# The first loads by pairs of heads, ten more idle products, and a new written order for the opening of an attention and feed-forward kernel

## The chip, the core and the metric

The kernel runs on one core of a Trainium2 chip. The core has five engines that each work through a queue of instructions in order: TensorE (PE, with its weight loads as PEld), VectorE (DVE), ScalarE (ACT), GpSimd (POOL), and SyncE (SP), which here only issues transfers. They meet through semaphores. The metric is the device time of one execution in microseconds (us), the median of several runs.

## The reference

Eight batches, eight heads, 576 tokens of 64 numbers. k and v are first averaged over groups of 8 tokens, so that each head has 72 keys and values. Behind the attention stands a feed-forward layer with a gate.

```python
k_p = k.reshape(B, H, 72, 8, D).mean(axis=3);  v_p = likewise
scores = (1 / sqrt(D)) * q @ k_p^T
attn = exp(scores - max);  attn = attn / (sum(attn) + 1e-9)
x = (attn @ v_p), heads side by side: 4608 tokens x 512
h = x @ w_in                      # 512 x 2048
g = h * clip(h + 3, 0, 6) / 6
out = g @ w_out                   # 2048 x 512
```

## The kernel before, in words

The 4608 tokens are cut into ten blocks (512, 256, 384, six of 512, 384). For a block, the feed-forward layer runs in 16 steps `f`, one for each 128 of the 2048 inner columns: `Step.h` (L782) forms h in PSUM, ScalarE and VectorE apply the gate (`relu`, `gate` L794, `hi`, `lo`), and `Step.out` (L813) adds the step's part of the result. Each product is split into high and low parts, three matmuls for one. While a block's steps run, the attention of the next block is laid between them. So almost all of the run is a stream of matmuls, and only the opening, in which the attention of block 0 is made with nothing to lay it beside, is different.

**The opening.** Block 0 is the first 512 tokens of batch 0, four tiles of 128 tokens: A is the tiles 0 and 128, B the tiles 256 and 384. Heads are taken in four pairs, and two pairs make a group `g` (0 or 1), so a tile has two sets of scores, 4 heads by 72 keys each.

- `load_first` issues the loads: four k of a pair each (L257), q of tile 0 and of tile 128 (L259), the 8 remaining keys' v (`vr`, L260), v of pairs 0 and 1 and of pairs 2 and 3 (L262), the two halves of the weights of step 0 (L653), and q of tokens 256 to 511 (L264) between these. Then come the weights of step 1, the k of batch 1 (`load_k`, L200), and, in `load_second`, batch 1's v (L375) and its remainder three times over (L377).
- `prep_k` (L214) sums 8 tokens of k on VectorE; ScalarE scales the sums into `kbd` (L222). The same function serves batch 1 with another `kbd`.
- `busy` (L270) forms idle products of the identity, which nothing reads: 13 ahead of the scores and 3 behind them.
- `FirstValues.heads` (L290) sums 8 tokens of v by products with the identity, 16 products; `FirstValues.rest` (L301, L303) does the remainder on GpSimd.
- `Scores`: `product` (L412) on TensorE; `top` (L416), the maximum, on VectorE; `exps` (L420), four exponentials with their sums, on ScalarE. The fourth set of A has `shift` (L427) and `total` (L433) on VectorE and one wide `exp` (L430) on ScalarE instead. `invert` (L436, L437) on VectorE; `divide` (L448, L454) on GpSimd or VectorE.
- `transposes_of_half` (L507, L509): six transposes of the weights for two tiles and one g, then a copy of the main part out of PSUM (L510, VectorE or ScalarE) and of the remainder (L511, ScalarE).
- `av` (L583): the product with the values for a pair of heads, then the split into `xhi` (L588) and `xlo` (L589).
- `prep(f, ...)`: the weights of a step are made out of 64-bit words: `scale` (L695) and `low` (L684) on ScalarE, `sign` (L689) and `join` (L700) on VectorE, `hi` (L723) on ScalarE, `lo` (L728) on VectorE. Those of steps 0, 1 and 2 fall into the opening.
- `pool_second` (L385) sums batch 1's v on VectorE, six instructions.

**What sets the order.** `ORDER` is a table: for each engine, the numbers of its instructions of the opening and the first steps behind it, in the order in which the engine is to run them (a number is the place of the instruction in the order of the program's text; for SP they are the loads). `put_in_order` chains them by `behind`, which adds an order with no semaphore. Each engine then takes its instructions strictly in that order; waits between engines follow from the data and the buffers.

On TensorE, the order before is: 13 idle products; the scores of A in the order tile 0 of g 1, tile 0 and tile 128 of g 0, tile 128 of g 1; 3 idle products; the value sums; transposes of g 0; the first scores of B; transposes of g 1; `av` of A; further scores of B between products of step 0; transposes and `av` of B, whose third product is the `av` at 34.07 us.

Of the kernel before, what the change touches and what calls it, by code (L numbers as in the profile page):

```python
# [17 lines left out]
P = 128  # L18
# [12 lines left out]

ORDER = {
    "PE": """
        0-12 17-18 13-16 19-45 50-53 56-57 46-49 54-55 60-63 58-59 64-68 78-79 69-71 80-85 88-89 72-74 86-87
        75-77 100-101 96-99 102-108 118-126 109-111 211-214 112-117 93-95 90-92 127-144 230-233 145-147 246-247
        148-156 166-171 157-159 163-165 266-267 160-162 193-195 184-189 172-180 190-192 196-198 181-183 218-223
        199-201 208-210 277-278 297-298 202-204 299 215-217 205-207 224-229 251-253 240-242 234-236 248-250
        243-245 237-239 254-259 279-281 260-262 268-270 263-265 274-276 315-316 282-287 306-308 288-296 334-336
        303-305 271-273 300-302 309-314 323-328 317-322 337-342 349-350 362-364 331-333 343-345 329-330 346-348
        354-356 365-367 357-359 368-376 385-387 360-361 380-381 351-353 382-384 388-390 377-379 391-393 419-421  # L40
        394-396 400-402 409-411 397-398 406-408 403-405 422-427 451-453 438-440 428-430 399 441-443 454-456
        431-433 416-418 457-462 444-446 412-415 479-481 466-468 434-437 476-478 469-472 447-450 463-465 482-493
        473-475 536-537 503-505 494-496 530-532 562-563 544-546 497-499 547-549 533-535 538-540 582-583 541-543
        500-502 512-514 509-511 550-555 515-517 506-508 556-558 518-523 576-578 559-561 564-569 579-581 524-526
        584-589 570-572 527-529 573-575
    """,
    "DVE": """
        3 2 1 0 4-8 87 11 15 9 12 17 16 10 18 13 19 14 20-21 23 22 24 26 34 28 40 64 29 25 61 32 30 33 62 36 35
        37 27 39 38 47 31 43-44 41 65 55 93 45 50 49 51 63 52-53 56 54 42 48 59-60 57-58 99 74 46 100 77 73 106
        76 75 79 81 78 82 111 80 107 121 86 108 83-84 112 67 110 85 113 90 88 109 89 68 94 114 91-92 115 131 96  # L50
        98 95 101 136 97 103 66 143 105 102 116 104 137 118 117 132 122 120 126 119 128 133 127 130 129 144 140
        123 138 147 139 142 141 72 149 145 70-71 146 124 69 152 125 135 148 151 150 154 156 134 159 153 157 155
        166 158 160-161 168 170 167 163 172 162 169 173 164-165 171 174-175 178-179 187 183 181 184-186 188 194
        176 189 182 177 190 199 191 180 200 192 201 193 195 197-198 202 196 203
    """,
    "Activation": """
        3 2 0-1 4-18 27 19 34 21 20 25 23 82 22 24 81 28-32 35-38 46 26 33 53 40-43 54 44 47-50 52 56 51 60 55
        39 59 69 89 61 57-58 45 88 74 96 95 71 67 70 75 68 97 104-107 98 72 76 79 73 80 77 108-111 86 78 83-84
        93 62 90 85 87 94 117-120 91 126-129 99 102 92 115 103 100 112 136 65 130 137 101 138-139 116 113 124
        121 114 125 122 140 123 143 66 63 131 64 132 134 144 135 153 133 145 141 147 142 150 148 146 154 151 149  # L60
        155 157 160 156 152 166 158 161 159 167 170-172 162-163 168 164 173 165 174 176 178 169 175 183 177
        180-181 179 187 186 184 188 185 194-197 189 202-205 198-199 182 200 208-211 190-191 201 206 192 207
        212-213 193
    """,
    "Pool": """
        0-1 12 2-3 18 4 7-8 10 5 9 6 14 13 16 15 17 11 19-20 24 21 23 22
    """,
    "SP": """
        2-3 1 0 4-5 8 6-7 14 9 11 10 22-24 21 20 13 12 15 18 16 19 25-26 28 31 17 27 32 34 33 29 41 30 44 51 35
        48 46 43 36 47 39 52 59 42 37-38 45 40 50 49 53-55 57-58 60 56  # L70
    """,
}

# [2 lines left out]
def attention_moe_kernel(  # L76
# [19 lines left out]
    nc = tc.nc  # L96
    NB, _, NPAIR, S = q.shape
# [5 lines left out]
    NG = NPAIR // 2  # L103
# [7 lines left out]
    for j, t in enumerate(starts):  # L111
        end, mine = t + BLOCKS[j], []
# [83 lines left out]
    kraw = {}  # L196
# [48 lines left out]
    def load_first():  # L245

        st = [stage(i) for i in range(16)]
        qs = [st[i].rearrange("p (c t) -> p c t", c=NPAIR) for i in (11, 4)]
        pieces[256], pieces[0] = [st[1:4], 0], [st[8:11], 0]
        vraw[0] = stages[3].rearrange("p a (c n) -> p (a c) n", a=2, c=NPAIR // 2)  # L250
        vraw[0, NPAIR] = st[5][:REM].rearrange("p (g n) -> p g n", g=NG)
        for t in tiles_of[0]:
            _, s0, _, _ = t[0]
            qtiles[t] = [qs[s0 // 256][:, :, s0 % 256 : s0 % 256 + P]]
        for p in range(NPAIR):
            kraw[0, p] = st[12 + p][:, :S]
            nc.sync.dma_start(kraw[0, p], k[0, p])  # L257
        for o in range(0, 256, P):
            nc.sync.dma_start(qs[0][:, :, o : o + P], q[0, :, :, o : o + P])  # L259
        nc.sync.dma_start(vraw[0, NPAIR], vr[0].rearrange("g r n -> r g n"))  # L260
        for p in range(0, NPAIR, 2):
            nc.sync.dma_start(vraw[0][:, p : p + 2], v[0, p : p + 2].rearrange("p r n -> r p n"))  # L262
        load_w(0, slice(0, 1))
        nc.sync.dma_start(qs[1], q[0, :, :, 256:512])  # L264
        load_w(0, slice(1, 2))

    def busy(n):

        for _ in range(n):
            nc.tensor.matmul(idle, ident, ident, start=True, stop=True)  # L270
# [585 lines left out]

    window.append(len(traced))
    load_first()
    load_w(1)
    for p in range(NPAIR):  # L860
# [237 lines left out]
```

## Time and profile before

| | us |
|---|---|
| median of 3 runs | 923.84 |
| the runs | 923.11 to 926.03 |
| the profiled execution | 923.03 |
| its span | 921.2 |
| TensorE busy | 908.1 (99%) |
| VectorE busy | 457.4 (50%) |
| ScalarE busy | 461.7 (50%) |
| GpSimd busy | 82.0 (9%) |

The span is the time from the first to the last instruction that the profiler saw; the run's own time is 1.8 us more. TensorE's share hides the opening: of the span's 40 slices (23 us each) only the first two and the last have TensorE under 90%.

### The profile page before, as it was taken

The page shows a single profiled execution, that of the slowest core. Times are in us where ns is not written, and L with a number is a line of the kernel's source. Part 1 is how long each engine was busy: PE and PEld are TensorE (multiplying, and loading weights), DVE is VectorE, ACT ScalarE, POOL GpSimd, SP SyncE. Part 2 cuts the span into 40 slices and gives each one's busy share as a digit, 9 for nine tenths or more (in the row PEclk, how much of TensorE's full clock was granted, in tenths as well). Part 3 has the DMA queues.
Part 4 walks back from the last instruction along what each step waited for, and adds up shares of the span by engine and source line. Part 5 has one row for each costly group of instructions (what it writes and reads, how often), then busy time and mean ns, then how long its engine had stood idle before and what let it go on. Part 6 is the DMA issues. An engine that isn't in the chain of part 4 may idle for free.

```text
span 921.2 us, 12671 instructions
## 1 busy us (share of the span) xinstructions
PE 908.1 (99%) x4548; PEld 776.8 (84%) x4548; DVE 457.4 (50%) x916; ACT 461.7 (50%) x1340; POOL 82.0 (9%) x167
## 2 busy tenths in 40 slices
PE   7899999999999999999999999999999999999998
PEld 7688889999888888888888888888888888888997
DVE  6999855475356333824356326633356234332322
ACT  6898665465355434633456335633545344333322
POOL 4100001021000100101011101110101001100000
PEclk9999999999999999999999999999999999999999
DMA  9960203050031002300042004100210010000100
GB/s 313 393 242 1 92 12 121 1 166 19 0 115 58 24 1 80 104 12 6 1 145 57 12 1 134 61 12 1 92 42 23 1 41 18 0 1 3 45 1 35
DMA packets 41935, 57.19 MB, mean 62 GB/s; under 512 B 7568, under 2 KB 23696, under 8 KB 41872
## 3 DMA queue, kind: packets, MB, share of 16 engines
q1 hardware_dynamic: 41728, 56.37, 19.0%
q8 instruction: 36, 0.59, 0.3%
q14 instruction: 27, 0.22, 0.1%
q10 hardware_dynamic: 144, 0.00, 0.0%
HBM read 46.93 MB, written 9.44 MB: 61 GB/s over the span
## 4 chain that ended last, share of the span: by engine, by line
PE 96%; DVE 2%; DMA 1%; SPq 0%; ACT 0%; issue 0%; DVEq 0%
PE pso L813 43%; PE psh L782 43%; PE psa L583 4%; PE psa L412 4%; PE psa L518 2%; DMA kst<-k_l 1%; PE psa L520 0%; DVE u L689 0%; ACT stage L420 0%; DVE u L700 0%; SPq L257 0%; DVE stage L448 0%; SPq L259 0%; DVE a L510 0%; SPq L262 0%
## 5 line engine op out<-in xcount | busy, mean ns | idle before, releaser
L782 PE MATMUL psh<-xhi,w 128*128 128x512 f32 (+2 forms) x1288 | 402.3, 372 | 0.0
L813 PE MATMUL pso<-w,ghi 128*128 128x512 f32 (+1 forms) x1184 | 367.0, 391 | 0.0
L782 PEld LDWEIGHTS psh<-xhi,w 128*128 128x128 f32 x1288 | 238.0, 188 | 36.1 <-issue 0.4
L813 PEld LDWEIGHTS pso<-w,ghi 128*128 128x128 f32 x1184 | 214.1, 188 | 36.0
L782 PE MATMUL psh<-xlo,w 128*128 128x512 f32 (+2 forms) x644 | 237.5, 369 | 0.0
L794 DVE SCALAR_TENSOR_TENSOR g<-g,psh 128x512 f32<-128x512 f32 (+2 forms) x161 | 101.4, 630 | 271.6 <-ACT g L790 270.4
L813 PE MATMUL pso<-w,glo 128*128 128x512 f32 (+1 forms) x592 | 225.9, 386 | 0.0
L790 ACT ACTIVATE g<-psh,small 128x512 f32<-128x512 f32 (+2 forms) x161 | 103.7, 644 | 209.7 <-PE psh L782 193.3
L782 PEld LDWEIGHTS psh<-xlo,w 128*128 128x128 f32 x644 | 121.3, 188 | 18.2
L802 DVE TENSOR_TENSOR glo<-g,ghi 128x512 fp32r<-128x512 f32 (+2 forms) x161 | 102.7, 638 | 62.1 <-ACT ghi L798 60.2
L813 PEld LDWEIGHTS pso<-w,glo 128*128 128x128 f32 x592 | 111.1, 188 | 21.7
L798 ACT CAST ghi<-g 128x512 fp32r<-128x512 f32 (+2 forms) x161 | 92.9, 577 | 70.6 <-DVE g L794 67.9
L420 ACT ACTIVATE e<-psa,mx 128x72 f32<-128x72 f32 x256 | 78.5, 322 | 50.8 <-DVE mx L416 50.1
L448 POOL TENSOR_TENSOR a<-e,sm 128x256 f32<-128x256 f32 x60 | 41.2, 687 | 517.2 <-PE pso L813 180.3
L420 ACT ACTIVATION_READ_ACCUMULATOR e<-psa,mx 128x1 f32 x256 | 52.8, 206 | 0.0
L416 DVE TENSOR_REDUCE mx<-psa 128x4 f32<-128x288 f32 x72 | 32.3, 454 | 29.2 <-PE psa L412 28.8
L412 PEld LDWEIGHTS psa<-kbd,qt 128*128 128x128 f32 x288 | 43.1, 189 | 4.2
L412 PE MATMUL psa<-kbd,qt 128*128 128x144 f32 x288 | 45.5, 285 | 0.0
L585 ACT COPY x<-psa 128x192 f32<-128x192 f32 (+7 forms) x60 | 23.0, 387 | 32.6 <-PE psa L583 32.4
L332 DVE TENSOR_REDUCE vsum<-vst 128x64 f32<-128x512 f32 (+1 forms) x36 | 37.8, 1068 | 2.3 <-DMA vst<-v_l 1.5
L436 DVE TENSOR_SCALAR sm<-sm 128x4 f32<-128x4 f32 x72 | 12.4, 176 | 48.7 <-ACT e L420 45.7
L529 ACT CAST ahi<-psa 128x256 fp32r<-128x256 f32 (+1 forms) x70 | 24.6, 353 | 18.8 <-PE psa L518 9.8
(93 smaller groups left out, 628.9 us busy)
## 6 DMA issues: line engine op xcount, KB each, us to landing
out<-o SPq DMA_DIRECT2D x35, 256.0 KB, 2.3
raw<-w_in_l SPq DMA_DIRECT2D x16, 512.0 KB, 8.4
raw<-w_out_l SPq DMA_DIRECT2D x16, 512.0 KB, 9.1
kst<-k_l SPq DMA_DIRECT2D x28, 288.0 KB, 3.2
qt<-q_l SPq DMA_DIRECT2D x28, 256.0 KB, 3.2
vst<-v_l SPq DMA_DIRECT2D x24, 256.0 KB, 3.0
vst<-vr_l SPq DMA_DIRECT2D x36, 64.0 KB, 1.9
stage<-k_l SPq DMA_DIRECT2D x4, 288.0 KB, 3.6
```

The lines of the kernel that those rows point to most:

```text
L332: nc.vector.tensor_reduce(out=vs[:n, p], in_=st[:n, : POOL * D].rearrange("p (o d) -> p d o", o=POOL), axis=AX.X, op=ALU.add)
L412: nc.tensor.matmul(to, qt[:, p, :], kbds[b % 2][:, p, :], start=r == 0, stop=r == last)
L416: nc.vector.tensor_reduce(out=self.mx, in_=self.ps, axis=AX.X, op=ALU.max, negate=True)
L420: nc.scalar.activation(self.e[:, h], self.ps[:, h], AF.Exp, bias=self.mx[:, h : h + 1], accum_out=self.sm[:, h : h + 1])
L448: engine.tensor_tensor(out=self.a[:, : 4 * D].rearrange("p (h s) -> p h s", h=4), in0=e[:, :, :D], in1=sm[:, :, None].broadcast_to([P, 4, D]),
L583: nc.tensor.matmul(ps, l, r, start=n == 0, stop=n == len(mms) - 1)
L782: nc.tensor.matmul(self.ps, l[f][:, c, :], r[:, c, :], start=c == 0 and i == 0, stop=c == NCC - 1 and i == 2)
L790: nc.scalar.activation(self.g, self.ps, AF.Relu, bias=half, scale=1.0 / (6.0 * WSCALE))
L794: nc.vector.scalar_tensor_tensor(out=g, in0=g, scalar=1.0, in1=self.ps, op0=ALU.min, op1=ALU.mult)
L798: nc.scalar.copy(self.ghi, self.g)
L802: nc.vector.tensor_tensor(out=self.glo, in0=self.g, in1=self.ghi.bitcast(F32), op=ALU.subtract)
L813: nc.tensor.matmul(pos, l, r[:, cols], start=f == 0 and i == 0, stop=f == NF - 1 and i == 2)
```

## The change

`load_first` takes q of the first 256 tokens by heads, where it took it by tokens: the k of pairs 0 and 1, the q of these pairs for all 256 tokens, the k of pairs 2 and 3, their q. The second `busy` makes 13 idle products where it made 3. And the whole table `ORDER` is another.

```diff
-        for p in range(NPAIR):
-            kraw[0, p] = st[12 + p][:, :S]
-            nc.sync.dma_start(kraw[0, p], k[0, p])
-        for o in range(0, 256, P):
-            nc.sync.dma_start(qs[0][:, :, o : o + P], q[0, :, :, o : o + P])
+        for g in range(NG):
+            mine = slice(2 * g, 2 * g + 2)
+            for p in range(NPAIR)[mine]:
+                kraw[0, p] = st[12 + p][:, :S]
+                nc.sync.dma_start(kraw[0, p], k[0, p])
+            nc.sync.dma_start(qs[0][:, mine], q[0, :, mine, :256])
...
     values.rest()
-    busy(3)
+    busy(13)
...
     "PE": """
-        0-12 17-18 13-16 19-45 50-53 56-57 46-49 54-55 60-63 58-59 64-68 78-79 69-71 80-85 88-89 72-74 86-87
+        0-12 15-16 21 13-14 22-23 17-18 24 19-20 25-26 34-49 54-55 50-53 64-65 68-69 56-59 62-63 76-78 66-67
+        60-61 88-89 27-28 74-75 70-71 29 72-73 90-93 30 79-84 94-95 85-87 31 98-99 96-97 110-111 32-33 106-109
...
     "DVE": """
-        3 2 1 0 4-8 87 11 15 9 12 17 16 10 18 13 19 14 20-21 23 22 24 26 34 28 40 64 29 25 61 32 30 33 62 36 35
+        0-5 87 6-9 15 11 10 16-17 12 18 14 19 13 21 23 22 24 20 34 29 25 40 27 26 93 28 55 35 56 32 36 30 37 43
...
     "Activation": """
-        3 2 0-1 4-18 27 19 34 21 20 25 23 82 22 24 81 28-32 35-38 46 26 33 53 40-43 54 44 47-50 52 56 51 60 55
+        0-3 82 81 4-18 27 19 21 20 34 25 24 53 26 54 22 28-31 23 35-38 32 46 40-43 33 47-50 56 44 39 60 52 88 59
...
     "Pool": """
-        0-1 12 2-3 18 4 7-8 10 5 9 6 14 13 16 15 17 11 19-20 24 21 23 22
+        0-1 17 12 11 2-3 8 7 4 10 5 9 6 13-14 18 16 15 19-20 22 24 21 23
...
     "SP": """
-        2-3 1 0 4-5 8 6-7 14 9 11 10 22-24 21 20 13 12 15 18 16 19 25-26 28 31 17 27 32 34 33 29 41 30 44 51 35
+        0-5 14 7 6 8-9 11 13 12 10 15 20 16 18 21 19 17 35 26 25 27 34 24 28 31 33 36 32 42 30 29 39 43 51 23 40
```

What the numbers stand for in the rows shown (places are counted from 0):

- **SP.** Before: four k, two q, v of pairs 2 and 3, vr, v of pairs 0 and 1, k of batch 1's pair 0 (number 14, place 9), the two weights of step 0 (9, 11), the second half of q (10), vr of batch 1 (22 to 24), its v, the weights of step 1 (13, 12). After: k, k, q, k, k, q, k of batch 1's pair 0 (place 6), v of pairs 0 and 1, vr, v of pairs 2 and 3, the weights of steps 0 and 1, and then the second half of q (place 14). The three loads of batch 1's vr go to places 27, 39 and 44, behind weights of steps up to 12.
- **PE.** After 13 idle products, the scores of A come as tile 128 and tile 0 of g 0, then tile 0 and tile 128 of g 1; six idle products (numbers 21 to 26) stand among them and behind them; then the value sums (34 to 49), transposes of g 0, and at once `av` of pairs 0 and 1 (64, 65, 68, 69). Products of step 0 (76 to 87) are spread over the scores, transposes and `av` that follow, with the other seven idle products (27 to 33).
- **DVE.** The reduction of batch 1's k (87) goes from place 9, behind all the maxima of A and the shift, to place 6, behind the maxima of g 0 (numbers 4 and 5). Sign and join of the weights of step 1 (55, 56) go from places 50 and 59 to 34 and 36. Of the six sums of batch 1's v (61 to 66), five stood ahead of the last copy of B (54); after, two do. The first gate (42) and the sign step of step 2's weights (60) stood behind that copy and now stand ahead of it.
- **Activation.** The two scalings behind that reduction (82, 81) go from places 26 and 29, ahead of B's exponentials, to places 4 and 5, ahead of A's.
- **Pool.** Three memsets (17, 12, 11) come ahead of the sums of vr (2 to 4).

## Rows read from the trace of the kernel before

**Rows 1.** Windows: length; busy us (instructions) of PE, PEld, DVE, ACT, POOL; PEclk; DMA; GB/s.

```profile
31.40:34.40 3.00, 1.10 (x8) 0.82 (x8) 3.00 (x6) 2.79 (x5) 1.14 (x3) 1.00 1.11 364
34.40:37.80 3.40, 3.40 (x11) 2.78 (x10) 2.88 (x4) 2.32 (x6) 0.00 (x0) 0.50 1.02 392
37.80:41.20 3.40, 3.40 (x22) 3.04 (x22) 3.15 (x5) 2.96 (x7) 0.00 (x0) 1.00 1.03 410
60.00:110.00 50.00, 50.00 (x233) 41.29 (x232) 46.55 (x67) 41.52 (x77) 0.00 (x0) 1.00 0.21 74
```

**Rows 2.** Timeline of TensorE: start, busy us, line, operation, count [idle before <-releaser].

```profile
7.61 2.20 PE L412 MATMUL psa<-kbd,stage 128*128 128x144 f32 x16
9.65 0.83 PE L270 MATMUL idle<-ident 128*128 128x128 f32 x6
12.13 3.84 PE L290 MATMUL psa<-stage,ident 128*128 128x128 f32 x32 [1.65 <-DMA stage<-v_l]
...
34.07 0.94 PE L583 MATMUL psa<-a,v 128*128 128x256 f32 x2 [0.98 <-DVE a L510]
```

**Rows 3.** Timeline of VectorE.

```profile
4.29 3.04 DVE L214 TENSOR_REDUCE stage<-stage 128x72 f32<-128x576 f32 x4 [4.29 <-DMA stage<-k_l]
8.87 1.68 DVE L416 TENSOR_REDUCE mx<-psa 128x4 f32<-128x288 f32 x4 [1.54 <-PE psa L412]
10.58 0.46 DVE L427 TENSOR_TENSOR stage<-psa,mx 128x288 f32<-128x288 f32 x1
12.85 0.75 DVE L214 TENSOR_REDUCE ksum<-kst 128x72 f32<-128x576 f32 x1 [1.81 <-DMA kst<-k_l]
...
27.58 0.17 DVE L436 TENSOR_SCALAR sm<-sm 128x4 f32<-128x4 f32 x1 [0.45 <-ACT stage L420]
...
33.33 0.68 DVE L510 COPY a<-psa 128x512 f32<-128x512 f32 x1
```

**Rows 4.** Windows: from the start to VectorE's last copy.

```profile
0.00:33.33 33.33, 24.67 (x156) 22.00 (x156) 25.05 (x60) 24.41 (x89) 12.79 (x29) 1.00 0.99 338
```

**Rows 5.** Timeline of SP's queue: start, us, line, transfer, count.

```profile
0.74 1.81 SPq L257 DMA_DIRECT2D stage<-k_l  x4
2.59 1.31 SPq L259 DMA_DIRECT2D stage<-q_l  x2
```

**Rows 6.** Issues near 0.7, 2.6 and 3.9 us: KB, us from issue to landing.

```profile
stage<-k_l SPq DMA_DIRECT2D x1, 288.0 KB, 2.8
...
stage<-k_l SPq DMA_DIRECT2D x1, 288.0 KB, 4.4
...
stage<-q_l SPq DMA_DIRECT2D x1, 256.0 KB, 5.0
```

**Rows 7.** Timeline of ScalarE.

```profile
9.36 0.32 ACT L420 ACTIVATE stage<-psa,mx 128x72 f32<-128x72 f32 x1 [1.34 <-DVE mx L416]
...
12.94 0.51 ACT L430 ACTIVATE stage<-stage 128x288 f32<-128x288 f32 x1
...
19.93 0.26 ACT L222 ACTIVATE kbd<-ksum 64x72 f32<-64x72 f32 x1
```

**Rows 8.** Timeline of VectorE, instructions that change their side of the last copy.

```profile
20.69 0.67 DVE L385 TENSOR_TENSOR stage<-stage 96x512 f32<-96x512 f32 x1
...
28.26 0.41 DVE L385 TENSOR_TENSOR stage<-stage 96x256 f32<-96x256 f32 x1
...
33.93 0.40 DVE L794 SCALAR_TENSOR_TENSOR g<-g,psh 128x256 f32<-128x256 f32 x1
...
35.73 1.21 DVE L689 SCALAR_TENSOR_TENSOR u<-raw,u 128x1024 uint32<-128x1024 uint32 x1
```

**Rows 9.** Timelines of VectorE and GpSimd, the sign step twice and a division.

```profile
16.09 1.14 DVE L689 SCALAR_TENSOR_TENSOR u<-raw,u 128x512 uint32<-128x512 uint32 x1
...
19.11 0.69 DVE L689 SCALAR_TENSOR_TENSOR u<-raw,u 128x512 uint32<-128x512 uint32 x1
...
16.60 1.09 POOL L448 TENSOR_TENSOR stage<-stage,sm 128x256 f32<-128x256 f32 x1
```

More of the change, by code (lines that the diff above doesn't have):

```diff
@@ L39 @@
[L39 to L43, printed above, removed]
@@ L44 @@
-        500-502 512-514 509-511 550-555 515-517 506-508 556-558 518-523 576-578 559-561 564-569 579-581 524-526
-        584-589 570-572 527-529 573-575
+        0-12 15-16 21 13-14 22-23 17-18 24 19-20 25-26 34-49 54-55 50-53 64-65 68-69 56-59 62-63 76-78 66-67
+        60-61 88-89 27-28 74-75 70-71 29 72-73 90-93 30 79-84 94-95 85-87 31 98-99 96-97 110-111 32-33 106-109
+        114-118 112-113 119-121 100-102 128-133 122-127 103-105 134-139 221-224 140-148 155-157 240-243 149-154
+        176-178 170-172 179-181 158-169 182-187 256-257 194-196 200-202 188-193 173-175 197-199 206-208 203-205
@@ new lines @@
+        276-277 218-220 231-233 209-211 228-230 212-214 225-227 234-236 215-217 253-255 250-252 237-239 287-288
+        261-263 258-260 244-249 278-280 307-308 284-286 309 289-291 281-283 264-275 310-312 292-300 313-315
+        325-326 316-318 301-303 319-321 304-306 322-324 344-346 359-360 341-343 336-338 333-335 339-340 327-332
+        347-349 367-369 350-355 364-366 356-358 361-363 375-377 370-371 378-383 372-374 387-389 384-386 395-397
+        407-409 392-394 401-406 390-391 398-400 410-412 419-421 413-415 429-437 451-453 422-425 438-440 461-463
@@ L46 @@
+        444-447 426-428 416-418 454-456 441-443 464-466 457-460 467-475 492-497 479-482 489-491 448-450 546-547
+        483-485 498-503 476-478 486-488 513-515 572-573 510-512 540-542 525-527 504-506 543-545 554-556 516-518
+        548-550 557-559 592-593 551-553 560-565 507-509 528-530 566-568 519-524 569-571 574-576 586-588 577-579
+        589-591 531-536 594-599 580-582 537-539 583-585
     """,
     "DVE": """
-        3 2 1 0 4-8 87 11 15 9 12 17 16 10 18 13 19 14 20-21 23 22 24 26 34 28 40 64 29 25 61 32 30 33 62 36 35
@@ L49 @@
[L49 to L53, printed above, removed]
@@ L54 @@
-        176 189 182 177 190 199 191 180 200 192 201 193 195 197-198 202 196 203
+        0-5 87 6-9 15 11 10 16-17 12 18 14 19 13 21 23 22 24 20 34 29 25 40 27 26 93 28 55 35 56 32 36 30 37 43
+        33 38 61 39 31 41 47 50 62 44 51 45 52 42 53 49 60 54 48 99 46 59 58 74 57 76-77 73 100 79 75 81 63 78
+        84 80 82 88 83 86 106 111 85 90 92 68 67 89 94 112 91 107 96 108 95 113 121 101 109-110 97 64 131 98 65
+        103 115 122 114 102 105 104 66 118 116 136 117 123 126 137 119 132 120 143 133 128 130 127 138 129 140
@@ L55 @@
+        71 144 142 139 145 135 69 72 146 70 147 141 149 124 148 134 152 150 125 151 154 153 156-157 159 155 166
+        158 163 160 162 164 161 168 165 172-173 170 167 169 175 171 174 176 178 187 177 179 183 188 184 181 194
+        189 185 180 182 186 190 199 191-192 195 193 200 197-198 196 201-203
     """,
     "Activation": """
-        3 2 0-1 4-18 27 19 34 21 20 25 23 82 22 24 81 28-32 35-38 46 26 33 53 40-43 54 44 47-50 52 56 51 60 55
-        39 59 69 89 61 57-58 45 88 74 96 95 71 67 70 75 68 97 104-107 98 72 76 79 73 80 77 108-111 86 78 83-84
@@ new lines @@
+        45 51 55 89 69 96 58 57 95 70-71 86 67 74 68 75 97 72 98 79 73 76 83 77 80 78 87 104-107 61-62 90 84
+        108-111 85 93 91 99 115 92 94 117-120 102 100 103 112 101 126-129 124 113 121 130 116 114 125 134 136
+        122 137 131 138 147 123 66 143 135 63 65 139-140 132 141 153 64 142 144 133 145 150 146 149 148 154-155
+        151 157 156 152 160 166 158 161 163 159 162 164-165 171-172 169-170 167 175 178 168 173 179 176-177 174
+        180-182 186 183 194-197 188 187 184 189 185 202-205 198-201 208-211 206 190 207 191 212 192 213 193
@@ L64 @@
     """,
     "Pool": """
-        0-1 12 2-3 18 4 7-8 10 5 9 6 14 13 16 15 17 11 19-20 24 21 23 22
+        0-1 17 12 11 2-3 8 7 4 10 5 9 6 13-14 18 16 15 19-20 22 24 21 23
     """,
     "SP": """
-        2-3 1 0 4-5 8 6-7 14 9 11 10 22-24 21 20 13 12 15 18 16 19 25-26 28 31 17 27 32 34 33 29 41 30 44 51 35
-        48 46 43 36 47 39 52 59 42 37-38 45 40 50 49 53-55 57-58 60 56
+        0-5 14 7 6 8-9 11 13 12 10 15 20 16 18 21 19 17 35 26 25 27 34 24 28 31 33 36 32 42 30 29 39 43 51 23 40
+        44 46-47 22 48 45 41 37 52 38 49 59 50 53-54 58 56-57 55 60
```

9 lines of the change are left out of this document (removed).

## The prediction

> **What bounds the kernel now.** I read the table by stretches first: in 60 to 110 us TensorE is busy for all 50.00 us [rows 1], and it stays so almost to the end. A change that touches only the opening can therefore move the end by what it moves the moment from which TensorE never waits again, and by what TensorE's clock does around it. TensorE's own order gives that moment: 34.07 us, when a product of attention weights with values (`av`, L583) starts after 0.98 us of waiting for a copy by VectorE [rows 2]. So I went to VectorE. That copy (L510) starts at 33.33 us [rows 3]. Up to there VectorE works 25.05 us [rows 4], so it is idle 33.33 - 25.05 = 8.28 us, and the rows say where: 4.29 for the first k, 1.54 for the first scores, 1.81 for a k of batch 1, 0.45 for exponentials [rows 3]; 0.19 is crumbs. From 12.85 us on it is idle for that 0.45 only. So TensorE waits on a queue that VectorE runs almost without a break. The end of the opening is VectorE's work ahead of its last copy, plus its idle time, plus 0.74 (from 33.33 to 34.07). This is the sum I make again for the changed kernel.
>
> One more row matters. Behind a stretch in which TensorE was busy only 1.10 of 3.00 us, the granted clock is 0.50, 1.2 GHz, from 34.4 to 37.8 us; TensorE is busy there for all 3.40 us [rows 1], so about 3.4 / 2 = 1.7 us were lost.
>
> **The loads.** From the start to 33.33 us the DMA share is 0.99, at 338 GB/s [rows 4]. A landing therefore moves by the bytes that are put ahead of it. Before, four k (288 KB each) come first, then two q (256 KB each) [rows 5]. The first k lands at 0.74 + 2.8 = 3.5 us; the last is issued from about 2.1 and lands at 2.1 + 4.4 = 6.5; the second q, from about 3.3, lands at 3.3 + 5.0 = 8.3 [rows 5, 6]. After, the order is k0, k1, q of pairs 0 and 1, k2, k3, q of pairs 2 and 3, then a k of batch 1. k0 still lands at 3.5. Up to the end of k2 stand 1120 KB, where the last k had 1152: 6.4. k3 has 256 KB more ahead than that last k, 0.262 MB / 338 GB/s = 0.8: 7.3. The last q has the same 1664 KB: 8.3. The runs of q in memory get twice as long (256 tokens for 128). No row separates the two lengths; the q are 0.52 MB, which take 1.55 us at the mean of 338 GB/s and 1.28 at 410, the fastest of the stretches shown [rows 1, 4], so 0 to 0.3 us may be gained, and I take 0. The k of batch 1 has 1152 KB less ahead of it, 1.18 MB / 338 GB/s = 3.5 us: its reduction started at 12.85 behind that landing [rows 3], so it now lands at 9.3. Values 0 and 1 have 352 KB less ahead, 1.1 us: 12.1 [rows 2] becomes 11.0. Three loads of v's remainder of batch 1 go behind weights, and two loads of w_1 go ahead of the second half of q, which lands 1.05 MB / 338 GB/s = 3.1 us later; its scores have no place in the sum below as long as VectorE is the later of the two.
>
> **The front of the opening.** The first scores do not gain from the earlier q: the idle products end at 7.6, where the scores start [rows 2], and the k and q needed land shortly before. TensorE's new order is scores of tile 128 (its four scores took 9.65 - 7.61 = 2.04, 0.51 each [rows 2]), one idle product (three took 0.83, so 0.28 each), scores of tile 0. VectorE's first maximum is that of tile 0, the second score in both orders; with an idle product ahead of it, it moves from 8.87 [rows 3] to 9.1. The four reductions of k take 0.75 each (3.04 / 4) [rows 3]: k0 and k1 end at 5.1, k2 runs from 6.45 to 7.2, k3 from 7.35 to 8.1. VectorE's next: two maxima (1.68 / 4 = 0.42 each), end 9.95; the reduction of batch 1's k, 0.75, which finds its load landed: end 10.7; two further maxima and the shift (0.84 + 0.46 [rows 3]): end 12.0.
>
> **The added wait.** In ScalarE's new order the two scalings into `kbd` of that same reduction (L222) stand ahead of all exponentials; before, they came at 19.93 us, behind those of the first half [rows 7]. ScalarE takes its queue in order, so they hold it until 10.7, and the exponentials start near 11.1 (two scalings of 0.26, less overlap) where they started at 9.36. They run 12.94 - 9.36 = 3.58 us [rows 7]: end 14.7. Queued behind them on ScalarE are the last exponential (0.51) and the weights of step 0. VectorE waits for them: its divisions of the third set of scores need the third set of exponentials, so it is idle from 12.0 to 14.75 but for 0.15. That takes the place of the 1.81 us for the load: the wait is moved, not removed. The price can't exceed what the hold itself is, 11.1 - 9.36 = 1.7; below nothing it can't go, since nothing on ScalarE becomes shorter.
>
> **The sum.** Idle time of VectorE after: 3.6 for k0, 1.35 for k2, 0.15 for k3, 1.0 for the scores, 2.6 for the exponentials, together 8.7 against 8.28. Beyond 14.75 I take none, as it had only 0.45 beyond 12.85; with as much again the sum is 0.45 higher, and I keep that for the range. Work ahead of the last copy: three sums of batch 1's v (L385) leave, about 0.67 + 2 x 0.41 = 1.49; a gate (0.40) and the sign step of w_2 (1.21) come in [rows 8]: 0.12 more. The rest is the same set in another order. So the last copy moves by 0.42 + 0.12, say **0.6 us later**, and with it the products behind it.
>
> The ten idle products cost nothing in that sum. Of the 13 that now follow the scores' start, six stand ahead of the value sums and seven behind the first `av`, where TensorE waits 1.65 and 0.98 us and more [rows 2]; VectorE is the cover. Without it they would cost 10 x 0.28 = 2.8 at most, which is the upper end; below nothing they reach only through the clock (rivals). The reorder behind 34 us I put at nothing: in 60 to 110 us VectorE has 46.55 and ScalarE 41.52 of 50.00 [rows 1], so the cover is 3.45 us thick. Were VectorE late behind it, TensorE would show waits there. GpSimd's memsets move to the front, before its first load, and cost nothing.
>
> One price inside the work I checked. The same VectorE step (L689) took 1.14 us at 16.09 and 0.69 at 19.11, and beside the first GpSimd was at its own division [rows 9]. In the new order that step falls near 16.8, again beside such divisions, so I keep 1.14. The Trainium skill (GPSIMD Engine Reference, section 1, Specifications) has GpSimd share VectorE's SBUF interfaces, so that steps with two SBUF inputs get in each other's way. By that rule the sum stands; were the slow step chance, it would be 0.45 less.
>
> **The clock.** The new order leaves TensorE a hole. The value sums start at 11.0, and their 32 records (3.84 us) [rows 2] end near 14.9. Then come transposes as the divisions allow, up to about 17.1, and the first `av` only behind the sign step (1.14) and the copy (0.68) [rows 3, 9], at 18.6. In these 3.7 us it is busy about 1 us, a lower share than in the stretch ahead of the fall before [rows 1], and none of the added products stands there. So I expect the clock to fall behind 17 us. Behind 27 us added products and weight products fill the gaps, and I expect no fall at 34. One fall for another: 1.7 us in both.
>
> So the profiled execution's 923.03 us becomes 923.6. The median of the runs shown, 923.84, lies 0.8 above the profiled one; on that footing I forecast **924.4 us**. A measurement of this kernel tells about 0.3% from no change, 2.8 us (921.1 to 926.6); this forecast is no change.
>
> **Rivals.**
> (a) The clock never falls: the hole is shorter than I think, and the later products hold it. For it: ten more products. Against: none of them in the hole. 924.4 - 1.7 = **922.7**.
> (b) Slower. The clock falls in the hole and again before 35 us, because products at half rate make VectorE late for the copies behind. It decides if the hole lasts from 14.9 to 18.6 and the products of tokens 256 to 511 still wait near 33 us. Price: 1.7 for the second fall and up to 0.8 of waits, 924.4 + 2.5 = **926.9**.
> (c) Faster. The reduction of batch 1's k gets into VectorE's idle time before 9.1, so that the exponentials start near 9.4. For it: 1.0 us of idle time there. Against: VectorE takes its queue in order, and two maxima stand ahead. It would give 1.5, and with a kept clock 1.7 more: 924.4 - 3.2 = **921.2**.
> (d) Nothing of it is seen: q by pairs comes earlier, nothing uses it, and the rest evens out: 923.8, inside the forecast's own range.
>
> **Chances.** Forecast with (d) 0.50; (a) 0.22; (b) 0.17; (c) 0.11. The forecast's own range is 923.2 to 925.4. To hold 8 of 10 the range takes in (a) and most of (b), the uncovered idle products lying at its upper end: 921.7 to 927.0. Faster by over 0.3% is half of (c) and a sliver of (a): 0.08. Slower is most of (b) and 0.02 for a late VectorE behind 60 us: 0.16. Same: 0.76.
>
> **What would show it.** ScalarE's first exponential near 11.1 behind the two scalings, not 9.4; VectorE idle from 12.0 to 14.7 waiting for ScalarE; the first `av` at 18.6; VectorE's last copy near 33.9; no waits of TensorE beyond 35 us; a granted clock of 0.50 behind 17 us. I am wrong in mechanism if the exponentials start at 9.4, if the last copy is not bound by VectorE's own queue, or if TensorE waits behind 40 us; wrong in size if the clock is low in two stretches or in none.

## The result

The changed kernel takes 926.64 us (median of 18 runs, 925.53 to 931.39) against 923.37 for the kernel before (18 runs beside it, 921.98 to 926.03). The ratio is 1.0042, with a 95% interval of 1.0033 to 1.0050: slower by 3.3 us in the medians and 3.9 by the ratio. Forecast was 924.4 and no change. The time lies in the range, but the sign is that of rival (b) (926.9), and (b)'s mechanism, two falls of the clock, shows in the profile below but, by their mean clocks, not in most executions. That the median comes within 0.3 us of (b)'s price is luck.

The profile after is of an execution of 930.33 us, with a span of 928.2. TensorE's timeline, with what it waited for:

```profile
2.38 5.83 PE L271 MATMUL idle<-ident 128*128 128x128 f32 x26 [2.38 <-POOL ident masks.py:199]
8.04 0.66 PE L413 MATMUL psa<-kbd,stage 128*128 128x144 f32 x4
...
20.02 1.19 PE L584 MATMUL psa<-a,v 128*128 128x256 f32 x2 [2.06 <-DVE a L511]
...
32.67 1.11 PE L508 MATMUL psa<-ident,stage 128*128 128x128 f32 x4 [2.83 <-POOL stage L449]
...
41.61 0.67 PE L584 MATMUL psa<-a,v 128*128 128x256 f32 x2 [0.88 <-DVE a L511]
...
146.45 0.73 PE L814 MATMUL pso<-w,ghi 128*128 128x512 f32 x2 [0.77 <-ACT o L820]
```

The wait for VectorE's last copy, which ended at 34.07 us [rows 2], ends at 41.61. A wait stands at 146.45 us, where the kernel before has none. The windows of the same execution:

```profile
20.00:25.00 5.00, 4.98 (x15) 4.17 (x16) 3.46 (x7) 3.23 (x5) 0.00 (x0) 0.50 1.04 397
25.00:29.60 4.60, 4.60 (x34) 4.28 (x32) 4.17 (x9) 4.27 (x22) 0.00 (x0) 0.99 1.03 410
29.60:32.67 3.07, 0.24 (x2) 0.00 (x0) 2.88 (x10) 3.07 (x19) 2.00 (x2) 0.87 1.05 367
32.67:38.50 5.83, 5.83 (x24) 5.46 (x25) 3.17 (x10) 2.60 (x4) 1.46 (x4) 0.50 1.06 357
```

TensorE runs at 1.2 GHz twice, each time behind a stretch in which it waited. ScalarE's timeline has the hold that the prediction named:

```profile
11.02 0.53 ACT L222 ACTIVATE kbd<-ksum 64x72 f32<-64x72 f32 x2 [2.76 <-DVE ksum L214]
11.46 0.30 ACT L421 ACTIVATE stage<-psa,mx 128x72 f32<-128x72 f32 x1
```

and VectorE's the idle time it makes, and the late copy:

```profile
9.45 0.82 DVE L417 TENSOR_REDUCE mx<-psa 128x4 f32<-128x288 f32 x2 [1.87 <-PE psa L413]
10.19 0.74 DVE L214 TENSOR_REDUCE ksum<-kst 128x72 f32<-128x576 f32 x1
...
15.19 0.24 DVE L437 TENSOR_SCALAR sm<-sm 128x4 f32<-128x4 f32 x2 [2.19 <-ACT stage L421]
...
40.77 0.69 DVE L511 COPY a<-psa 128x512 f32<-128x512 f32 x1
```

The executions of a kernel differ in how long TensorE's clock was low, and this one is not typical. Of the 18, it is one of three with a mean granted clock of 0.993 or 0.994 (928.9 to 931.4 us); eleven have 0.997 or 0.998 (925.5 to 926.95), four 0.996 (926.8 to 928.2). So the first run below is the changed kernel once more.

### The profile page after: what moved, and what is told of

Same layout as the page of the kernel before. It is cut to its first block, busy times and chain, and to the rows that moved or that the text cites. A ratio compares the mean times of both kernels' runs of the same rounds, so it can differ in the third digit from the quotient of the medians.

```text
span 928.2 us, 12714 instructions
## 1 busy us (share of the span) xinstructions
PE 914.0 (98%) x4568; PEld 782.3 (84%) x4568; DVE 459.0 (49%) x916; ACT 461.2 (50%) x1340; POOL 81.8 (9%) x167
## 4 chain that ended last, share of the span: by engine, by line
PE 97%; DVE 1%; ACT 1%; POOL 0%; issue 0%; POOLq 0%; ACTq 0%
PE psh L783 43%; PE pso L814 43%; PE psa L584 5%; PE psa L413 4%; PE psa L519 2%; PE idle L271 1%; ACT stage L421 0%; PE psa L521 0%; PE psa L508 0%; DVE u L690 0%; POOL stage L449 0%; DVE mx L417 0%; DVE a L511 0%; DVE u L701 0%; DVE stage L455 0%
## 5 line engine op out<-in xcount | busy, mean ns | idle before, releaser
L783 PEld LDWEIGHTS psh<-xlo,w 128*128 128x128 f32 x644 | 121.6, 189 | 18.2
L437 DVE TENSOR_SCALAR sm<-sm 128x4 f32<-128x4 f32 x72 | 13.0, 183 | 53.1 <-ACT e L421 48.5
```

The costliest lines, as they stand in the source:

```text
L783: nc.tensor.matmul(self.ps, l[f][:, c, :], r[:, c, :], start=c == 0 and i == 0, stop=c == NCC - 1 and i == 2)
```

## The experiments

Ratios are to the kernel before, run beside each; the changed kernel stands at 1.0042. "Held" means that TensorE never fell to 1.2 GHz in the opening of the profiled execution.

**e1, the changed kernel again** (no edit).

> The changed kernel once more, for a second profile, since the first shows TensorE at half rate in two stretches (18.2 to 25.1 and 31.9 to 38.7 us) and 930.3 us, while most of its executions lie at 925.5 to 927. If the clock is the whole cause of the loss, an execution near 926 still shows a second stretch or a longer one. If waits are, it shows one stretch, and TensorE's idle time up to 45 us is over that of before by the difference. If it is the idle products, the idle time is that of before and TensorE's busy time is higher by about 2.5 us.

One execution: 927.48 us, a mean clock of 0.996, one stretch at 1.2 GHz, 18.3 to 25.1. The idle time up to 45 us is 9.12 us (before 9.40), TensorE's work 2.9 us more at full rate. By these numbers alone the idle products were my suspect.

**e2, without the ten.**

```diff
-    busy(13)
+    busy(3)
     "PE": 24 to 33 leave the table
```

> The second run of idle products is 3 again: the first three keep their places among the scores, the ten others leave every place. Theory 1, the ten cost their own time because TensorE itself ends the opening: 923.4 to 924.4, 2.2 to 3.2 us under the changed kernel. Theory 2, VectorE's and ScalarE's new orders make the loss and the ten only fill waits: no change, 926 to 927. Theory 3, the ten hold the clock: slower, 928 to 930, with a longer stretch at 1.2 GHz.

925.82 us, 1.0042 (1.0029 to 1.0055). Theory 1 and theory 3 both half true: at a clock of 0.996 the executions are 1.7 us faster (925.77 against 927.43 on average), but four of five are at 0.996 and none higher, where the changed kernel had eleven of 18 at 0.997 or more. The sum is nothing.

**e3, the scalings back.**

```diff
     "Activation"
-        0-3 82 81 4-18 27 19 21 20 34 25 24 53 26 54 22 28-31
+        0-18 27 19 21 20 34 25 24 53 26 54 22 82 81 28-31
```

> The two scalings into kbd of batch 1 go back behind all exponentials of A, on ScalarE alone; all else is the changed kernel. ScalarE's exponentials should start at about 9.9 in place of 11.5. Theory 2a, this hold carries through to the end of the opening: 1.0 to 1.6 us faster than the changed kernel, about 925.2. Theory 1 or 2b (sign and join ahead of B's inversions): what is gained at 10 us is lost again in the waits behind, 926.2 to 926.9.

925.05 us, 1.0032 (1.0021 to 1.0044): 0.9 us less by the ratio and 1.0 at a clock of 0.998 (925.09 against 926.13), the low end of theory 2a, though the interval overlaps that of the changed kernel. The exponentials start at 9.29 us, 2.2 earlier. In the profiled execution the clock held, and yet VectorE's last copy starts at 34.91, 1.6 us later than before. The hold is not the whole. But the edit also makes a wait: VectorE's next reduction of batch 1's k waits 1.29 us, to 22.88, for the scalings that now come late.

**e4, sign and join back.**

```diff
     "DVE"
-        ... 93 28 55 35 56 32 36 ... 39 31 41 47 ... 42 53 49 60 54
+        ... 93 28 35 32 36 ... 39 31 41 55 47 ... 42 53 56 49 60 54
     "Activation"
-        ... 88 59 45 51 55 89
+        ... 88 45 51 55 59 89
```

> Sign and join of the weights of step 1 go back on VectorE: sign behind the copy of B's first transposes, join between the two divisions of B's last set, as before the change; ScalarE's hi of step 1 goes behind the copy of B's last remainder. Theory 2b, they hold back the inversions of B's first two sets, so that GpSimd's division starts late and the transposes wait (2.83 us in the profile after): 1.5 to 2.5 us faster, near 924.5. Theory 1: TensorE's chain behind 33 us takes its time either way, 926 to 927; or slower by up to 1 us, as step 1 gets its weights later.

930.1 us, 1.0088 (1.0073 to 1.0104): 4 us slower, and theory 2b falls. The wait on GpSimd's division is shorter (1.12 us), but five others come behind it, four of them of 0.37 to 1.03 us, the last ends at 38.97, and the clock is down from 19.7 to 23.1 and again from 36.7 to 43.5 us, where TensorE has no wait to hide it.

**e5, ScalarE's last places back.**

```diff
     "Activation"
-        208-211 206 190 207 191 212 192 213 193
+        208-211 190-191 206 192 207 212-213 193
```

> ScalarE's last places only: the scalings of block 0's results (L820) come ahead of the relu and the hi of block 1's step 2, as before the change; all else is the changed kernel. Theory, this is the wait of 0.77 us that TensorE shows at 146.4 us, at the end of block 0, released by L820, which the kernel before does not have: the wait goes and the time falls by 0.7 to 0.8 us, to a ratio of 1.0034 to before against 1.0042. Rival, the wait is hidden or only moves to the next result bank: no change.

928.34 us, 1.0059 (1.0044 to 1.0073). The wait of 0.77 us is gone, as expected, but two others are there; TensorE's waits from 45 to 300 us:

```profile
PE psh L783 <- DVE g L795: 2.1, 2, 1.1
```

The order of the instructions behind the table isn't written in the program; it is planned when the kernel is built. This edit changed it: in the trace 76 of VectorE's 916 instructions differ from those in the same place of the changed kernel, the first of them the 212th, where the table has 204. The rest of the table's edits here left VectorE's and ScalarE's order behind the table alone, but for e7, which contains this one. So 0.77 us is the wait's size, and that it can be had back was not shown.

**e6, the hole filled.**

```diff
     "PE"
-        50-53 64-65 68-69 ... 27-28 74-75 70-71 29 72-73 90-93 30 ...
+        50-53 27-33 64-65 68-69 ... 74-75 70-73 90-93 ...
```

> The seven idle products that stand behind the first av go ahead of it, into TensorE's wait of 2.06 us for VectorE's copy; all else is the changed kernel. Theory, an idle product costs its 0.21 us unless it stands in a wait whose end it doesn't move: seven times 0.21 is 1.5 us less, a ratio of 1.0026; and if the hole is what lowers the clock at 18 us, up to 1.7 to 2.5 us more. Rival, the places where they stood were covered too: TensorE's waits behind grow by the 1.5 us that its work there falls, and nothing changes but the clock.

927.33 us, 1.0046 (1.0033 to 1.0059): the rival. The wait ahead of the first `av` falls from 2.06 to 0.49 us, the clock holds there, and the wait for GpSimd's division grows from 1.53 (e1) to 2.96, with the clock down from 29.5 to 33.0. Its execution also has a wait of 1.19 us at 159 us that no other has.

**e7, three edits together** (e3, e5, e6).

> Three edits of the changed kernel together: the two scalings into kbd behind A's exponentials, the seven idle products in the hole, ScalarE's last places as before. If they add up: 1.0 + 1.5 + 0.75 us less than the changed kernel, a ratio of 1.0007, and under 1.0 where the clock holds. If the hole's end was set by the scalings, the seven products in the now shorter hole delay the first av and give back up to 1 us: 1.0018.

926.85 us, 1.0039 (1.0026 to 1.0052): they don't add up. It has e5's planned waits (1.7 us), and its clock is down from 27.2 to 34.0.

**e8, the loads alone**, on the kernel before.

```diff
     load_first as in the change
     "SP"
-        2-3 1 0 4-5 8 6-7 14
+        3-4 1 0 5 2 8 6-7 14
```

> The kernel before with one part of the change: q of the first 256 tokens comes in two transfers by pairs of heads, with 1024-byte runs for 512-byte ones, in the same places of SP's queue; the table is that of before but for these numbers. Theory, the queue is full either way and the first products wait for the idle products: no change, within 0.3 us. Rival, the longer runs move faster: the loads behind land up to 0.3 us earlier, and 0.1 to 0.3 us are gained. The time outside the span, 1.83 us before and 2.1 after, shows whether it belongs to this load.

921.9 us, 0.9994 (0.9985 to 1.0002): no change, and 1.82 us outside the span.

**e9, the sum away from GpSimd.**

```diff
     "DVE"
-        33 38 61 39 31 41 47
+        33 38 39 31 41 61 47
```

> One edit of the changed kernel: the first sum of batch 1's v on VectorE (L386, 1024 columns) goes from beside GpSimd's division for B's first set to behind the copy of B's first transposes. Theory, the two slow each other down (the sum took 1.63 us for 1.20 before, the division and its rest 1.9 to 2.3 for about 1.0), and TensorE's wait on that division (1.53 to 2.83 us near 31 us) is their price: it falls by about 1 us, and the time by 0.6 to 1.0, to a ratio of 1.0034. Rival, VectorE has the same work to do ahead of its last copy, so the wait comes back there: no change, 1.0042.

926.87 us, 1.0047 (1.0031 to 1.0062). The collision is real, the gain is not. In e1, VectorE and GpSimd:

```profile
30.80 1.63 DVE L386 TENSOR_TENSOR v<-v 128x1024 f32<-128x1024 f32 x1
...
31.32 1.32 POOL L455 TENSOR_TENSOR stage<-stage,sm 128x96 f32<-128x96 f32 x1
```

and in e9:

```profile
30.92 1.21 DVE L386 TENSOR_TENSOR v<-v 128x1024 f32<-128x1024 f32 x1
...
29.52 0.36 POOL L455 TENSOR_TENSOR stage<-stage,sm 128x96 f32<-128x96 f32 x1
```

But in e9 VectorE's own division of the remainder now stands beside GpSimd's and takes 0.67 us in place of 0.40, and the sum is still ahead of the last copy, which starts at 36.31.

**e10, ten more idle products alone**, on the kernel before.

```diff
-    busy(3)
+    busy(13)
     "PE"
-        21-23 24-39
+        21-33 34-49
```

> The kernel before with one part of the change: 13 idle products where it makes 3, all in front of the value sums, where TensorE waits 1.65 us for v. Ten take about 2.15 us (two records of 0.11 each). Theory, a product in a wait is free up to the wait's length, and the value sums are not what the order behind waits for: 0 to 0.5 us, a ratio of 1.0000 to 1.0005, with the wait of 1.65 gone in the profile. Rival, each costs its time wherever it stands: 2.15 us, 1.0023.

921.9 us, 0.9995 (0.9986 to 1.0004). They fill the wait for v and cost nothing:

```profile
9.56 3.06 PE L270 MATMUL idle<-ident 128*128 128x128 f32 x26
12.53 3.84 PE L290 MATMUL psa<-stage,ident 128*128 128x128 f32 x32
```

The value sums start 0.4 us later [rows 2], and TensorE's idle time up to 45 us falls from 9.40 to 7.60.

**e11, idle products in four later waits**, on the kernel before with e8's loads; `busy(12)`, two ahead of the last scores of B, three, two and two ahead of the first `av`, the remainder's last transpose and the third `av` of B.

> The kernel before with q by pairs of heads, and nine idle products in four of TensorE's waits: two ahead of the last scores of B (0.82 us), three ahead of the first av of B (1.16), two ahead of the last transposes of the remainder (0.92), two ahead of the third av (0.98). Each group is shorter than its wait. Theory, they cost nothing and keep the clock from falling at 34 us in the executions in which it falls: the same as before where it doesn't fall, 1.7 us less where it does, a ratio of 0.998 to 1.000. Rival, they delay what stands behind: 1.9 us more, 1.002.

922.08 us, 0.9995 (0.9987 to 1.0004). None of its 11 executions shows a clock under 0.999, where 11 of the 23 of the kernel before beside them stand at 0.998, so they do hold it. In the profiled execution, the slowest of the 11 (923.27), the last wait ends at 35.12, 0.95 us later than in e8; whether that holds for the others, and takes the gain back, is not shown.

**e12, the ten doubled.** `busy(23)`, each of the ten twice in its place.

> Each of the ten products that the change adds is made twice; all else is the changed kernel. Theory 1, they add to TensorE's work and the waits do not shrink by as much: TensorE's busy time at full rate grows by 2.1 us, its idle time up to 45 us stays within 0.5 us of 9.1 to 9.7, and the time grows by 1.5 to 2.1 us, less what the clock gives. Rival, they stand in waits: the idle time falls by 2.1 us, the time stays.

926.77 us, 1.0049 (1.0036 to 1.0062): nearly the rival. TensorE works 2.5 us more than the mean of 908.9 of the changed kernel's two profiles, and its idle time up to 45 us is 7.75 where it was 9.12 and 9.74. At the same clock of 0.998 the executions are 0.7 us slower (926.82 against 926.13), and the mean clock rises from 0.9967 to 0.9980. So theory 1 falls: the products go into waits for the most part, and the rest is of the size that the higher clock gives back.

**e13, no remainder sums.** `FirstValues.rest` is empty; 2 to 6 leave the table of GpSimd.

> The changed kernel without GpSimd's five steps on v's remainder of batch 0 (L302, L304); the last 8 pooled values of batch 0 are left out of block 0 with them. Theory, VectorE's work ahead of its last copy is 1.6 to 2.2 us longer than before the change because other steps of it now lie beside GpSimd's: the step of 96 columns that took 0.97 us (0.40 before) and the sign step (1.10) lie beside these five, so VectorE's busy time up to the last copy falls from 26.7 to 27.2 to about 26.0, and the time by about 0.8: a ratio of 1.0035. Rival, these steps are slow by themselves or the copy waits for something else: no change, 1.0042 to 1.0049.

925.84 us, 1.0030 (1.0017 to 1.0042): 1.1 us less by the ratio, but its interval ends just at the point of the changed kernel and overlaps its interval, so the time alone doesn't show it.

**e14, the same on the kernel before.**

> The control: the kernel before without the same five steps. There the sign and join steps at 16.1 and 17.8 us lie beside them (1.14 and 1.07 us for 0.69 and 0.67 of their kind later). If VectorE's queue ends the opening before too, it gets 0.8 us shorter and the time falls by as much: a ratio of 0.9991. If it falls by as much as the changed kernel does, these five steps are not the difference between the two, and what is left of it lies beside GpSimd's divisions.

923.33 us, 1.0003 (0.9991 to 1.0015): no change, neither of the two outcomes that I wrote down. The join step did get shorter (0.68 us for 1.07); the sign step stayed at 1.10, beside GpSimd's division. In the profiled execution VectorE is busy 24.66 us up to its last copy, 0.4 less, but waits 0.89 us for the transposes ahead of its first copy, behind a stretch in which the clock was low (13.3 to 16.7 us). At equal clocks there is no change either: 921.87 against 921.93 us on average at 1.000. So by the medians these five steps cost the changed kernel 1.1 us and the kernel before nothing; the step from one to the other is not clear of noise, and what VectorE does in the traces has to carry the argument. VectorE's work up to its last copy, by the window from the start in e12 and e13 (compare [rows 4]: 25.05):

```profile
0.00:36.21 36.21, 29.29 (x196) 26.62 (x196) 27.24 (x60) 25.92 (x94) 13.10 (x29) 1.00 0.98 341
```

```profile
0.00:33.64 33.64, 26.17 (x176) 23.11 (x176) 25.48 (x59) 25.48 (x93) 9.12 (x24) 1.00 0.98 357
```

**e15, what cost nothing, together**: e8 and e10.

> The two parts of the change that cost nothing, on the kernel before with its own table: q by pairs of heads, and ten more idle products in front of the value sums. Each alone stood at 0.9994 and 0.9995. If they add up: 0.9990, 921.5 us where before is 922.5. If both were noise: 1.0000.

922.71 us, 0.9997 (0.9987 to 1.0006): no gain shown. "Both were noise" fits best, though 0.9990 lies in the interval too. No version tried is shown to be faster than the kernel before.

## Why the prediction was wrong

**The frame of the sum was right.** I held that the end moves by what TensorE's last wait moves, and by the clock. The profiled executions bear it out. Take from each time the end of the last wait in the opening, TensorE's waits behind 45 us, half of its time at 1.2 GHz behind the last wait, and the time outside the span; the rest should be one number.

| | us | last wait ends | waits behind | clock behind | outside span | rest | VectorE to its last copy: busy, idle |
|---|---|---|---|---|---|---|---|
| before | 923.03 | 34.07 | 0 | 1.71 | 1.83 | 885.4 | 25.05, 8.28 |
| e8 | 921.92 | 34.17 | 0.5 | 0 | 1.82 | 885.4 | 25.15, 8.29 |
| e10 | 923.34 | 34.33 | 0 | 1.71 | 1.84 | 885.5 | 25.03, 8.57 |
| after | 930.33 | 41.61 | 0.8 | 0 | 2.13 | 885.8 | 25.93, 14.84 |
| e1 | 927.48 | 38.69 | 0.8 | 0 | 2.18 | 885.8 | 26.69, 11.17 |
| e3, held | 924.39 | 35.73 | 0.8 | 0 | 2.09 | 885.8 | 27.15, 7.76 |
| e9 | 925.87 | 37.13 | 0.8 | 0 | 2.07 | 885.9 | 27.20, 9.11 |
| e12, held | 925.77 | 37.04 | 0.8 | 0 | 2.07 | 885.9 | 27.24, 8.97 |
| e13, held | 922.83 | 34.47 | 0.8 | 0 | 1.83 | 885.7 | 25.48, 8.16 |

The other eight lie between 885.6 and 886.3, so the frame holds to 0.9 us. What has to be explained is the last wait: I had it 0.6 us later, and with the new table and all its steps it is 1.7 (e3) to 7.5 us later (after).

**The step that failed is VectorE's time between the exponentials and its last copy.** I let the exponentials release VectorE at 14.75 us, put 0.12 us more work behind, took no idle time ("Beyond 14.75 I take none") and so had the last copy near 33.9. The second of VectorE's small adds (L437, before L436) stands at that release in the new order, and behind the landing of batch 1's k in the old one. Split there, the profiles read:

| | released | work behind it | idle behind it | last copy |
|---|---|---|---|---|
| before | 13.59 | 19.29 | 0.45 | 33.33 |
| after | 15.19 | 20.04 | 5.54 | 40.77 |
| e1 | 15.21 | 20.65 | 2.00 | 37.86 |
| e9 | 14.24 | 20.54 | 1.53 | 36.31 |
| e12, held | 15.29 | 20.63 | 0.29 | 36.21 |
| e13, held | 14.01 | 19.63 | 0.00 | 33.64 |

The windows behind the release, of the kernel before and of e1 (VectorE's is the third pair):

```profile
13.59:33.33 19.74, 15.11 (x98) 12.63 (x96) 19.29 (x51) 17.56 (x58) 7.62 (x14) 1.00 1.05 370
```

```profile
15.21:37.86 22.65, 16.83 (x90) 13.74 (x90) 20.65 (x48) 19.01 (x61) 7.21 (x12) 0.85 1.05 378
```

So in e1 the work is 1.36 us more where I had 0.12, and the idle time is 2.00 us where I had none. In both profiles of the changed kernel itself the idle time is the larger miss, and none of its 18 executions has the clock at 1.000.

**The work.** I wrote "The rest is the same set in another order." The set was right: three sums left, a gate and a sign step came. The time was not, because other steps of the same set now lie beside GpSimd's. I had checked one such step (L689, 1.14 us) and kept its price, rightly: it took 1.10. But it is only one place. In e1, VectorE's small add ahead of the fourth set's reciprocal, that reciprocal, and its division of the remainder:

```profile
16.03 0.59 DVE L437 TENSOR_SCALAR sm<-sm 128x4 f32<-128x4 f32 x1
...
16.70 0.17 DVE L438 RECIPROCAL sm<-sm 128x4 f32<-128x4 f32 x1
...
17.30 0.97 DVE L455 TENSOR_TENSOR stage<-stage,sm 128x96 f32<-128x96 f32 x1
```

and GpSimd:

```profile
15.98 0.61 POOL L449 TENSOR_TENSOR stage<-stage,sm 128x256 f32<-128x256 f32 x1
16.56 0.54 POOL L302 TENSOR_TENSOR stage<-stage 32x128 f32<-32x128 f32 x1
17.06 0.52 POOL L455 TENSOR_TENSOR stage<-stage,sm 128x96 f32<-128x96 f32 x1
17.55 0.61 POOL L304 TENSOR_TENSOR vrem<-stage,small 32x256 f32<-32x256 f32 x1
```

An add of 4 columns (0.14 us before) starts just behind the start of GpSimd's division and ends with it; the division of 96 columns (0.40 before) ends about when the second of GpSimd's steps beside it does. The reciprocal of the same 4 columns, beside GpSimd's next step, is not longer. Added up over the steps that stand ahead of the last copy in both kernels, durations are 0.9 us longer in e1 than before: the longer ones are 0.57, 0.45, 0.43 and 0.40, with 0.42, 0.39 and 0.34 the other way. The rest of the 1.36 is the change of the set and less overlap between neighbours. e13 shows how much hangs on GpSimd: without five of its steps that division takes 0.67 us, the sign step 0.68, and VectorE's work behind the release is 19.63 us, 0.9 to 1.0 less than in e1, e9 and e12. Of this, 0.4 is the sign step, whose price stood before the change too.

VectorE's busy time from the start, 27.24 us in e12, overstates this. Of the 2.2 us over the kernel before, 0.5 to 0.7 is one more add of 4 columns, drawn out beside GpSimd's first sums of the remainder:

```profile
12.90 0.88 DVE L437 TENSOR_SCALAR sm<-sm 128x4 f32<-128x4 f32 x1 [0.51 <-ACT stage L421]
15.29 0.17 DVE L437 TENSOR_SCALAR sm<-sm 128x4 f32<-128x4 f32 x1 [1.51 <-ACT stage L421]
```

It took 0.17 us in e13 and stands in a wait that ScalarE's exponentials end, at 15.29, whether it is short or long. So it moved nothing, and turned idle time into busy time.

The Trainium skill (SBUF — State Buffer, section "SBUF: two separate sides") says that a GpSimd step and a VectorE step in a 2-port mode, or with two SBUF inputs against a GpSimd step that reads SBUF, share a pair of ports: the one that starts first has it for its whole instruction, and the other blocks. The trace agrees in that the add, started 0.05 us behind the division, ends 0.03 us behind it; in which mode an add with one input ran, no run here shows.

**The idle time behind the release.** In e1, 1.99 of the 2.00 us is waits of VectorE at 22.5 to 25.5 us for ScalarE's casts of products and for TensorE's scores, while TensorE ran at 1.2 GHz:

```profile
22.52 0.42 DVE L590 TENSOR_TENSOR xlo<-psa,xhi 128x256 fp32r<-128x256 f32 x1 [0.49 <-ACT xhi L589]
...
24.23 0.42 DVE L590 TENSOR_TENSOR xlo<-psa,xhi 128x256 fp32r<-128x256 f32 x1 [0.68 <-ACT xhi L589]
25.47 0.46 DVE L417 TENSOR_REDUCE mx<-psa 128x4 f32<-128x288 f32 x1 [0.82 <-PE psa L413]
```

In e12 and e13, where the clock held, 0.29 and nothing are left. So the clock that I priced as lost TensorE time was paid a second time by the queue that TensorE feeds. No run changes the clock alone, so this is read from the traces. In the execution of 930.33 us GpSimd adds to it. Its division, beside VectorE's sum of 1024 columns, took 1.95 us, for 0.64 in e1, where the sum was drawn out instead (1.63, here 1.22), and TensorE waited 2.83 us for it:

```profile
30.67 1.95 POOL L449 TENSOR_TENSOR stage<-stage,sm 128x256 f32<-128x256 f32 x1 [10.93 <-DVE sm L438]
```

**The release** came 0.4 us later than the 14.75 that I had in e1, since I took the first scores' start (7.6) as fixed. It is not. The idle products ahead of them begin at 1.2 GHz, 0.21 us from record to record, and go on at 0.11 when the clock has risen, at 5.5 us in e13 and only behind the last of them in e1:

```profile
2.37 5.87 PE L271 MATMUL idle<-ident 128*128 128x128 f32 x26 [2.37 <-POOL ident masks.py:199]
```

```profile
2.38 4.65 PE L271 MATMUL idle<-ident 128*128 128x128 f32 x26 [2.38 <-POOL ident masks.py:199]
```

The first scores start at 8.08 us in e1 and 6.87 in e13. In the nine profiles that keep the hold of the exponentials, the release follows them by 7.13 to 7.25 us. In the six with the old table the same add starts at 13.59 to 13.98, whenever the scores start, since it stands behind a load. So the change made the opening depend on when the clock first rises, by up to 1.2 us; of the distance between the last copies of e13 and e1, 1.2 us is this and not the edit.

**The clock.** That it falls in the hole, behind 17 us, was right: 18.2 us. "One fall for another: 1.7 us in both" was not right for the executions profiled: it stays down for 6.8 us (18.3 to 25.1 in e1) where before it was 3.4, and in the one of 930.33 us, as by their mean clocks in two more of the 18, it falls again. But ten of the 18 have a mean clock of 0.998, that of the profiled execution before, and for these it may have held. By my own list two low stretches make the forecast wrong in size. The mean granted clock of the changed kernel is 0.9967; of 29 executions of the kernel before in the last comparison, 12 are at 1.000 and 11 at 0.998. At equal clock, 0.998, the changed kernel averages 926.13, and the kernel before 923.2 to 923.6 in the three comparisons with eight or more such executions. So most of the difference, some 2.7 us, is not in the clock's mean, as far as times of separate comparisons can be set against each other.

**The ten idle products** at nothing: right in the sum (e2, e10, e12), by two effects that cancel in the changed kernel and by the wait for v in e10.

**The added wait.** Right: exponentials at 11.46 us (11.1 forecast), VectorE idle 0.64 + 2.19 (2.6). Its price, 0.9 to 1.0 us by e3, lies within my bound of 1.7.

**The reorder behind 34 us** at nothing: wrong by 0.77 us. ScalarE's table puts scalings of block 0's results (L820) behind the relu and the `hi` of block 1's step 2, and TensorE waits for such a bank at 146 us. By my own list, a wait behind 40 us makes the forecast wrong in mechanism. I had looked at busy shares at 60 to 110 us; the table reaches to 146.

**The loads**: the value sums start at 11.34 us without a wait for v (11.0 forecast), batch 1's k is no longer waited for, and q by pairs is worth nothing (e8). All right.

For e1, whose clock of 0.996 four of the 18 executions share, the terms are, against the profile before: last wait +4.62 (release 1.62, idle behind it 1.55, work behind it 1.36, copy to product 0.09), the wait behind the table (at 143.5 us here) +0.8, outside the span +0.35, rest +0.39, less 1.71 for the fall that no longer lies behind the wait: +4.45, which is 927.48 - 923.03.

**What stays open.** Where the 0.3 us outside the span come from: every version with the new table has 2.07 to 2.18 except e13 (1.83), every version with the old one 1.77 to 1.84. The 0.4 us in the rest. How much of the time, and not only of VectorE's work, GpSimd's five steps cost: the 1.1 us of e13 are not clear of noise. How a typical execution of the changed kernel, at a clock of 0.998, splits: none was profiled. And whether a plan behind the table that keeps e5's edit without its two waits would give the 0.77 back; none was tried.

## What to carry to other kernels

When the bound is one engine's queue, an order of the same steps is not the same time: list what every step will have beside it on GpSimd, and price all of them, not the one that caught the eye. Split busy time at the waits: a step that is slow ahead of a wait for something else costs nothing. A low clock costs twice where the engine that sets the end waits for the slowed one. A wait on a load hides when the clock rises; take the load's wait away, and the opening may follow the clock. And where an order is written only up to some point, look at its far end too, and at what is planned behind it.

## What the runs showed of the hardware

Beside GpSimd, small steps of VectorE were drawn out as much as large ones: an add of 4 columns took 0.59 us where it took 0.14, a division of 96 columns 0.97 for 0.40, a sum of 1024 columns 1.63 for 1.20, while a reciprocal of 4 columns kept its 0.17 (e1). It goes both ways: GpSimd's own division of 96 columns took 1.32 us in e1 for 0.36 in e9, and its division of 256 columns 1.95 (after) for 0.64 (e1). Nine idle products in four waits came with a clock of 0.999 or more in 11 of 11 executions (e11), where the kernel before beside them had 12 of 23. The first 26 records of idle products took 4.65 us in e13 and 5.87 in e1, by when the clock first rose.
